# Moving the tiles behind the small triangle by 64 bytes in an attention and feed-forward kernel

## The chip, the cores and the metric

The kernel runs on one core of a Trainium2 chip. The metric is the time of one execution on the device in microseconds; the kernel before was run three times, and the median counts.

## What is computed

Windowed attention with sink tokens over 4 batches of 8 heads, 768 positions and 64 channels, followed by a feed-forward layer over the 3072 tokens that result (512 to 2048 to 512 channels):

```python
scores = scale * np.matmul(q, k.transpose(0, 1, 3, 2))
keep = is_sink | in_window                  # 4 sinks, window 128
scores = np.where(keep, scores, -1000000000.0)
a = np.exp(scores - np.max(scores, axis=-1, keepdims=True))
a = a / (np.sum(a, axis=-1, keepdims=True) + 1e-09)
x = np.matmul(a, v)                         # heads put side by side: [3072, 512]
h = x @ w_in
sp = np.maximum(h, 0.0) + np.log1p(np.exp(-np.abs(h)))
out = (h * erf(sp)) @ w_out
```

## The kernel before

**Tiling.** The tokens are worked on in 12 groups of 256. For each group four pairs of heads go through attention (48 steps), and the result, transposed, is the input of the feed-forward layer: a tile of 128 partitions with 4 blocks of 256 tokens. A group's hidden layer is made in 16 blocks of 128 channels, and each block's activation goes at once into the output product of its group. Attention of later groups is interleaved with the feed-forward work of earlier ones. The order is written out by hand: a loop over slots in which every step has a priority, from a table of offsets, and a few order-only dependencies between instructions of one engine.

**Two kinds of feed-forward products.** The first group is computed in plain float32: `xf` times `wf` (L767) and `gf` times `wf` (L813). From the second group on every operand is split into a high and a low part of a float32 format that TensorE takes in one pass (`F32R`), and three of the four part-products are summed. In the hidden product (L771, 2112 matmuls) the weights `wt` are loaded as the stationary operand, 128 columns of 512 bytes per partition, and 256 columns of `xh` or `xl` stream past them. In the output product (L816, L817, L818, 336 matmuls each) 128 columns of the activation `g` are the stationary operand, and 512 columns of `wt` stream past. A load of the next stationary operand runs beside the matmul before it. Stationary slices begin at multiples of 512 bytes from the start of their tile, and so do the streamed ones.

**Where tiles stand.** A tile pool takes its space at the end of what was opened before, each tile behind the one before it. The weights' pool comes first: 33 buffers of 4096 bytes per partition. Directly behind it stands `pers`, whose first tile is `tri` (the small triangle, a mask of 64 bytes in a tile of 192), then `kq` (11520 bytes), `vz` (8192) and `pst` (4608). Then come the raw inputs (2048, and three of 1536), then the pool `work`: four buffers `u` of 2048, two of `pa` with 2560, two of `pz` with 2048, two of `xh` (and `xf`) with 4096, `r` with 2048, two of `g` (and `gf`) with 4096 and two of `xl` with 4096; at the end the small pool of sums. All pieces from `kq` to `xl` are multiples of 64 bytes.

**Around the change.** `tri` is written once by two compares on VectorE at the start and read by `copy_predicated` in every step's scores. From step 15 on the probabilities go through memory for their transposition: `turn` (in the weights' pool) to `pd` to `pa` (L498), four transfers a step in pieces of 32 elements, issued by SyncE; GpSimd then prepares `pa` and `pz` (L509, L513, L522), and TensorE multiplies them with the values (L563).

Of the kernel before, what the change touches and what calls it, by code (L numbers as in the profile page):

```python
# [19 lines left out]
P = 128  # L20
# [42 lines left out]
def kernel(  # L63
# [74 lines left out]
    def fast_path():  # L138
        with ExitStack() as st:
            pers = st.enter_context(tc.tile_pool(name="pers", bufs=1))  # L140
# [40 lines left out]
            set_mask(mask0)  # L181
            set_mask(mask1)

            tri = pers.tile([P, 192], mybir.dt.int8, name="tri")[:, :64]
            nc.vector.tensor_scalar(tri[:64], rf[:64, :64], float(P), None, op0=ALU.is_ge)
            nc.vector.tensor_scalar(tri[64:], rf[64:, 64:128], float(P), None, op0=ALU.is_lt)

# [637 lines left out]
    def general_path():  # L825

        NT_S = S // P
        with ExitStack() as st:
# [71 lines left out]
            with tc.tile_pool(name="g_one1", bufs=1) as one, tc.tile_pool(name="g_work1", bufs=2) as work:  # L900
# [3 lines left out]
                with tc.For_i(0, B, 1) as b:  # L904
                    for gb in range(GPB):
# [25 lines left out]
                        for i in range(2):  # L931
# [3 lines left out]
                            )  # L935

    fast_path()
    ok = nc.values_load(flagi[0:1, 0:1], min_val=0, max_val=1)
    with tc.If(ok == 0):
# [31 lines left out]
```

## Time and profile before

| | us |
|---|---|
| median of three runs | 712.26 (711.40 to 714.54) |
| the profiled execution | 710.78 |
| its span, first to last instruction | 708.8 |
| TensorE busy | 681.0 (96%) |
| TensorE weight loads busy | 564.1 (80%) |
| VectorE busy | 550.0 (78%) |
| ScalarE busy | 494.0 (70%) |
| GpSimd busy | 297.8 (42%) |
| mean granted clock of TensorE | 0.992 |

A share of busy time is a mean over the span. The stage up to 100 us loads the inputs and works on the first group in plain float32; from there to about 640 us attention and feed-forward work are mixed, and the rest is feed-forward work alone. Weight loads overlap matmuls, and a matmul's length runs from its start to the modelled end of its pipeline; so matmuls overlap as well, and the distance between two starts is shorter than a matmul's length.

### The profile page before, as it was taken

What the parts mean: (1) busy time and instruction counts of PE and PEld (TensorE: products, weight loads), DVE (VectorE), ACT (ScalarE), POOL (GpSimd) and SP (SyncE); (2) the same over time, 40 slices, a digit from 0 to 9 for tenths busy, and PEclk for the clock granted to TensorE, in tenths of its full rate; (3) what the DMA queues carried; (4) which work ended last, traced back from release to release, by engine and by line L of the source; (5) the groups of instructions that cost most, each with busy time, mean ns of one, the idle gap of its engine ahead of it and who ended that gap; (6) DMA issues with size and microseconds to landing.
All of it is one profiled execution on the core that took longest, in us unless ns stands there. A gap on an engine that the chain in (4) does not pass through costs nothing. (4 is left out here: it accounts for less than half of the span.)

```text
span 708.8 us, 16156 instructions
## 1 busy us (share of the span) xinstructions
PE 681.0 (96%) x5515; PEld 564.1 (80%) x5515; DVE 550.0 (78%) x1473; ACT 494.0 (70%) x1157; POOL 297.8 (42%) x501
## 2 busy tenths in 40 slices
PE   6789999999999999899999999999999999999997
PEld 3566566687888888788788888888888888889895
DVE  6979998787889889788898588788798687754352
ACT  4777777986984867476677586686578567586572
POOL 3512410234445545554555455455464337342221
PEclk9989999999999999999999999999999999999999
DMA  7999410202216454653564354453553543220001
GB/s 174 296 325 318 177 31 17 63 16 50 63 35 121 108 113 94 139 102 73 123 119 83 71 122 82 99 120 75 119 103 78 101 95 71 44 68 1 30 1 35
DMA packets 246858, 70.10 MB, mean 99 GB/s; under 512 B 214704, under 2 KB 238896, under 8 KB 246768
## 3 DMA queue, kind: packets, MB, share of 16 engines
q1 hardware_dynamic: 246208, 68.92, 41.8%
q8 instruction: 46, 0.75, 0.4%
q14 instruction: 44, 0.36, 0.2%
q10 hardware_dynamic: 560, 0.07, 0.1%
HBM read 50.27 MB, written 18.42 MB: 97 GB/s over the span
## 5 line engine op out<-in xcount | busy, mean ns | idle before, releaser
L771 PE MATMUL h<-xh,wt 128*128 128x256 f32 x1408 | 271.2, 283 | 1.2 <-DVE u L793 1.2
L771 PEld LDWEIGHTS h<-xh,wt 128*128 128x128 f32 x1408 | 223.4, 188 | 15.6 <-issue 7.8
L771 PE MATMUL h<-xl,wt 128*128 128x256 f32 x704 | 197.0, 280 | 0.3 <-DVE xl L583 0.3
L801 POOL TENSOR_TENSOR g<-u,g 128x512 fp32r<-128x512 f32 x84 | 113.6, 1353 | 176.4 <-DVE g L800 161.5
L789 ACT ACTIVATE u<-r 128x512 f32<-128x512 f32 x288 | 163.3, 623 | 20.4 <-DMA out_dram<-ot 5.5
L793 DVE SCALAR_TENSOR_TENSOR u<-u,u 128x512 f32<-128x512 f32 x168 | 136.2, 811 | 14.5 <-ACT u L789 1.4
L771 PEld LDWEIGHTS h<-xl,wt 128*128 128x128 f32 x704 | 132.4, 188 | 7.0 <-issue 2.8
L816 PE MATMUL o<-wt,g 128*128 128x512 f32 x336 | 133.2, 396 | 0.7 <-DVE g L800 0.6
L817 PE MATMUL o<-wt,g 128*128 128x512 f32 x336 | 132.2, 393 | 0.0
L818 PE MATMUL o<-wt,g 128*128 128x512 f32 x336 | 129.4, 396 | 1.7 <-POOL g L801 1.5
L426 ACT ACTIVATE pst<-pst,neg 128x144 f32<-128x144 f32 x192 | 77.4, 405 | 65.3 <-DVE neg L422 65.2
L793 DVE SCALAR_TENSOR_TENSOR u<-u,h 128x512 f32<-128x512 f32 x84 | 56.7, 675 | 50.6 <-ACT u L789 46.3
L784 ACT ACTIVATE r<-h 128x512 f32<-128x512 f32 x96 | 56.9, 593 | 45.3 <-PE h L771 34.4
L522 POOL TENSOR_SCALAR_AFFINE_SELECT pz<-pa 64x256 f32<-64x256 f32 (+1 forms) x96 | 47.5, 495 | 67.3 <-ACT pa L484 66.0
L816 PEld LDWEIGHTS o<-wt,g 128*128 128x128 f32 x336 | 63.1, 188 | 14.5 <-ACT u L789 1.3
L818 PEld LDWEIGHTS o<-wt,g 128*128 128x128 f32 x336 | 61.8, 188 | 15.9 <-POOL g L801 3.0
L817 PEld LDWEIGHTS o<-wt,g 128*128 128x128 f32 x336 | 63.1, 188 | 10.3 <-issue 0.3
L786 ACT ACTIVATE r<-r 128x512 f32<-128x512 f32 x96 | 60.6, 631 | 2.7
L785 ACT ACTIVATE r<-r 128x512 f32<-128x512 f32 x96 | 60.6, 632 | 2.5
L800 DVE CAST g<-u 128x512 fp32r<-128x512 f32 x84 | 37.5, 447 | 25.0 <-PE o L818 21.5
L513 POOL COPY pz<-pa 64x256 f32<-64x256 f32 x66 | 31.9, 484 | 56.3 <-DMA pa<-pd 55.5
L522 POOL TENSOR_SCALAR_AFFINE_SELECT pa<-pa 64x256 f32<-64x256 f32 (+1 forms) x96 | 47.7, 497 | 4.9
(99 smaller groups left out, 915.1 us busy)
## 6 DMA issues: line engine op xcount, KB each, us to landing
pd<-turn SPq DMA_DIRECT2D x33, 320.0 KB, 2.6
pa<-pd SPq DMA_DIRECT2D x132, 80.0 KB, 2.6
ws<-in_moe_w_in_dram SPq DMA_DIRECT2D x16, 512.0 KB, 6.0
ws<-in_moe_w_out_dram SPq DMA_DIRECT2D x16, 512.0 KB, 8.6
out_dram<-ot SPq DMA_DIRECT2D x24, 256.0 KB, 2.4
v<-in_v_dram SPq DMA_DIRECT2D x56, 96.0 KB, 2.5
kq<-in_k_dram SPq DMA_DIRECT2D x144, 32.0 KB, 2.0
kq<-in_q_dram SPq DMA_DIRECT2D x144, 32.0 KB, 2.2
```

What stands on the lines that cost most here:

```text
L426: mark["e", s] = nc.scalar.activation(y, y, AF.Exp, bias=d["neg"][:, i, h : h + 1], scale=-1.0, accum_out=d["sum"][:, i, h : h + 1])
L522: nc.gpsimd.affine_select(out=out, in_=x, pattern=[[0, 2], [0, 2 - i0], [-sg, HP]], compare_op=op, fill=0.0, base=0, channel_multiplier=sg,)
L771: last = nc.tensor.matmul(o, wt[NC * j + c][:, p, fs], xt[e][:, c, :], start=(m == 0), stop=(m == len(ops) - 1))
L784: nc.scalar.activation(r, h, AF.Tanh, bias=b_t, scale=0.5)
L785: nc.scalar.activation(r, r, AF.Square, bias=b_v, scale=-0.5)
L786: nc.scalar.activation(r, r, AF.Square, bias=b_r)
L789: sq = nc.scalar.activation(u, r, AF.Square, bias=b_a[i], scale=CS)
L793: pr = nc.vector.scalar_tensor_tensor(out=acc, in0=u, scalar=CC[i] * CS**2, in1=x, op0=ALU.add, op1=ALU.mult)
L801: nc.gpsimd.tensor_tensor(gl, acc, gh.bitcast(F32), op=ALU.subtract)
L816: behind(nc.tensor.matmul(o, gh[:, ws], wt[16 + f][:, 0, :], start=(f == 0), stop=False))
L817: nc.tensor.matmul(o, gh[:, ws], wt[16 + f][:, 1, :], start=False, stop=False)
L818: nc.tensor.matmul(o, gl[:, ws], wt[16 + f][:, 0, :], start=False, stop=(f == NF - 1))
```

## The change

The tile that holds the small triangle takes 256 bytes per partition in place of 192. The slice that is used of it stays the first 64 bytes. All tiles behind it stand 64 bytes further on; the weights' buffers, which lie ahead of it, stay.

```diff
-            tri = pers.tile([P, 192], mybir.dt.int8, name="tri")[:, :64]
+            tri = pers.tile([P, 256], mybir.dt.int8, name="tri")[:, :64]
```

## Rows read from the trace of the kernel before

**Rows 1.** The page's busy time: engine, us, share of span, instructions.
```profile
PE 681.0 (96%) x5515; PEld 564.1 (80%) x5515; DVE 550.0 (78%) x1473; ACT 494.0 (70%) x1157; POOL 297.8 (42%) x501
```

**Rows 2.** Busy time by stage, with granted clock, DMA share and GB/s behind.
```profile
100.00:200.00 100.00, 97.16 (x728) 75.04 (x727) 81.05 (x216) 83.20 (x195) 29.62 (x52) 1.00 0.17 40
...
400.00:500.00 100.00, 100.00 (x881) 87.25 (x878) 81.39 (x229) 72.17 (x169) 50.45 (x87) 1.00 0.46 96
...
600.00:700.00 100.00, 100.00 (x734) 88.52 (x733) 52.92 (x111) 63.97 (x121) 29.02 (x31) 1.00 0.11 27
```

**Rows 3.** TensorE's waits, longest first: us in total, times, longest us.
```profile
PE av L563 <- POOL pa L522: 5.2, 6, 1.9
PE tqk L351 <- DMA k_early<-in_k_dram: 4.4, 2, 3.8
```

**Rows 4.** Instructions of L767 and L813: shortest, median, longest ns, first and last start.
```profile
L767 PE MATMUL h<-xf,wf x128: 379/379/796, 25.8 to 93.6; 128*128 128x256 f32 x128
...
L813 PE MATMUL o<-wf,gf x96: 590/592/697, 53.9 to 147.4; 128*128 128x512 f32 x96
```

**Rows 5.** TensorE in order of time near 70 us: start us, us together, instruction.
```profile
69.83 1.67 PE L767 MATMUL h<-xf,wf 128*128 128x256 f32 x7
```

**Rows 6.** Instructions of L771, as in rows 4.
```profile
L771 PEld LDWEIGHTS h<-xh,wt x1408: 186/188/192, 102.8 to 694.2; 128*128 128x128 f32 x176
L771 PE MATMUL h<-xh,wt x1408: 276/278/683, 102.8 to 694.4; 128*128 128x256 f32 x176
...
L771 PE MATMUL h<-xl,wt x704: 276/278/388, 103.3 to 694.2; 128*128 128x256 f32 x176
```

**Rows 7.** TensorE in order of time, a hidden product at 383 us.
```profile
382.71 0.39 PE L771 MATMUL h<-xh,wt 128*128 128x256 f32 x2
...
383.73 0.28 PE L771 MATMUL h<-xh,wt 128*128 128x256 f32 x1
```

**Rows 8.** TensorE in order of time, a hidden product at 652 us.
```profile
651.69 0.40 PE L771 MATMUL h<-xh,wt 128*128 128x256 f32 x2
...
652.75 0.28 PE L771 MATMUL h<-xh,wt 128*128 128x256 f32 x1
```

**Rows 9.** Groups by line, 651.46 to 652.5 us: busy us, mean ns, idle before.
```profile
L771 PE MATMUL h<-xh,wt 128*128 128x256 f32 x6 | 1.2, 281 | 0.0
...
L771 PEld LDWEIGHTS h<-xh,wt 128*128 128x128 f32 x6 | 0.9, 190 | 0.0
```

**Rows 10.** Instructions of L816, L817 and L818, as in rows 4.
```profile
L816 PEld LDWEIGHTS o<-wt,g x336: 186/188/192, 156.1 to 702.7; 128*128 128x128 f32 x168
L816 PE MATMUL o<-wt,g x336: 388/390/505, 156.2 to 703.0; 128*128 128x512 f32 x168
...
L817 PEld LDWEIGHTS o<-wt,g x336: 186/188/193, 156.2 to 703.0; 128*128 128x128 f32 x168
L817 PE MATMUL o<-wt,g x336: 388/392/505, 156.4 to 703.2; 128*128 128x512 f32 x168
...
L818 PE MATMUL o<-wt,g x336: 388/394/503, 156.6 to 703.4; 128*128 128x512 f32 x168
```

**Rows 11.** TensorE in order of time, an output product at 308 us.
```profile
306.64 0.39 PE L816 MATMUL o<-wt,g 128*128 128x512 f32 x1
...
309.39 0.28 PE L771 MATMUL h<-xh,wt 128*128 128x256 f32 x1
```

**Rows 12.** TensorE in order of time, an output product at 162 us.
```profile
161.05 0.40 PE L816 MATMUL o<-wt,g 128*128 128x512 f32 x1
...
163.15 0.39 PE L817 MATMUL o<-wt,g 128*128 128x512 f32 x1
```

**Rows 13.** Two last matmuls of a sequence by line, and the loads behind them.
```profile
L818 PE MATMUL o<-wt,g 128*128 128x512 f32 x1 | 0.4, 388 | 0.0
301.95 0.53 PEld L563 LDWEIGHTS av<-pa,v 128*64 128x64 f32 x12 [2.38 <-POOL pa L522]
...
L818 PE MATMUL o<-wt,g 128*128 128x512 f32 x1 | 0.4, 397 | 0.0
330.84 0.42 PEld L563 LDWEIGHTS av<-pa,v 128*64 128x64 f32 x8 [0.36 <-issue]
```

**Rows 14.** The page's DMA issues: KB each, median us to landing.
```profile
pa<-pd SPq DMA_DIRECT2D x132, 80.0 KB, 2.6
```

## The prediction

> **What bounds the kernel now.** I read the share of busy time first, then the table by stage, then TensorE's waits. TensorE is busy for 681.0 of the 708.8 us of the span, the next engine for 550.0 [rows 1]; from 100 us on it is busy for 97 to 100 us of every 100, at the full granted clock of 1.00, which is the 2.4 GHz level [rows 2]. Its longest wait by name adds up to 5.2 us in six pieces [rows 3]. So the time is the number of matmuls times the distance from one start to the next, and what a start-to-start gains or loses is passed on almost whole. The change touches no instruction. It can only act through how long an instruction takes on operands that stand 64 bytes further on.
>
> **Where the operands stand.** The 33 weight buffers have 4096 bytes each, so all start at one place modulo 512, and the small triangle's tile follows directly behind them, at that same place. From there to the feed-forward inputs it is 192 bytes for the triangle, 11520 (kq), 8192 (vz), 4608 (pst), 2048 and 4608 (the raw tiles), 8192 (u), 5120 (pa), 4096 (pz): 48576 = 95 x 512 - 64. The hidden product's moving inputs xh and xl, and the output product's stationary tile g, thus stand 64 bytes short of the weights' place; with 256 in place of 192 they stand on it. What each product reads beside what changes from -64 to 0 (inputs streaming past weights) and from +64 to 0 (weights streaming past g).
>
> **What the two products cost now.** I measure against plain float32 on the same engine: 256 columns take 379 ns and 512 take 592 [rows 4], 213 ns for 256 columns, and seven such matmuls in 1.67 us start (1670 - 379) / 6 = 215 ns apart [rows 5]. The split products pass a column in half that time, so without any stall 512 columns would take 379 ns and start 215 ns apart, 256 would take 379 - 107 = 272.
> The hidden product takes 276 ns at its shortest, 278 in the median [rows 6]. It runs at one of two even paces for many matmuls in a row: nine starts in 383.73 - 382.71 = 1.02 us, 113.3 ns each, and nine in 652.75 - 651.69 = 1.06 us, 117.8 each [rows 7, 8]; in the second the matmul itself lasts 281 and the loads of xh's weights 190 in the mean instead of 188 [rows 9]. The median halfway between 276 and 281 says that each pace has about half of the 2112 matmuls. The faster pace is above what 256 columns need, since a load of 128 columns takes as long as they do and only starts with the matmul before; it is the floor here. The slower pace costs 4.5 ns x 1056 = 4.8 us.
> The output product's three lines take 388 at the shortest and 390, 392 and 394 in the median [rows 10]. Twelve start in 309.39 - 306.64 = 2.75 us, 229.2 ns each; in another stretch nine in 163.15 - 161.05 = 2.10 us, 233.3 each [rows 11, 12]. Over the unstalled 215 that is 14 ns each, 14.1 us for 1008 matmuls. So some 19 us of the span are stalls of reading. Whether those come from the place is the whole question.
>
> **The change, part by part.** Removed and added: no instruction, no wait, no transfer. The triangle's own two writes and the predicated copies read 64 bytes as before: nothing.
>
> Place of an operand taken by itself. The hidden product's stationary operand stands on the weights' place, the output product's 64 bytes short of it, and both load in 188 ns in the median, between 186 and 193 [rows 6, 10]. In plain float32 the moving operand stands 64 bytes short (xf) or on the place (wf), and 592 is 379 + 213 without a remainder [rows 4]. By these rows the place alone costs nothing. For the split products the rows have each moving operand at one place only, and the excess per 256 columns is 4 to 9 ns at either (276 and 281 over 272 there; 388 and 397 over 379 for twice the columns here). I take 0; the ends are in the next step.
>
> Place of two operands to one another, when a load runs beside a matmul. This no row shows at another distance than 64. Two rows bear on it from the side: matmuls that end a sequence, beside which no load runs. One took 388 ns, with no load for 2.38 us; another took 397, with no load for 0.36 us [rows 13]. Matmuls with a load beside them take 388 at the shortest and 390 to 394 in the median [rows 10], so they are no longer. So most of the stall is there without the neighbour that the change would move, and I take 0. Against it speaks the slower pace, where the load is lengthened too, 190 for 188 [rows 9]: the two streams do meet somewhere. So both ends stay open: below, all 19 us gone; above, the slowest paces seen everywhere, 4.5 ns for the other 1056 hidden matmuls (4.8 us) and 233.3 - 229.2 = 4.1 ns for 1008 output matmuls (4.1 us), 8.9 us.
> The Trainium skill, TensorE: Matmul & The Clock Gate, Part 2, says that the streamed operand and the weight load have a read port each and that loading takes nothing from the running matmul. By that rule the relative place is worth 0; the matmuls without a load beside them agree with it (388 and 397), the lengthened load of the slower pace does not.
>
> Tiles that transfers write. The transposed probabilities (pa), the raw inputs and the copies of the values move by 64 bytes as well, and SyncE's queue issues the same transfers in the same order. A pa transfer lands in 2.6 us in the median [rows 14], behind it GpSimd prepares the tile, and TensorE waits for that for 5.2 us in all [rows 3]. If landing gets shorter, at most those 5.2 us are to be had; the same 5.2 us taken again is my bound for a loss. I take 0, because six waits in 33 steps mean that the transfer is nearly always early.
> [...]
>
> Vector, scalar and GpSimd work keeps its shapes; its tiles move together, and only weight splitting and the turn tile meet an operand that stays. TensorE's 97 to 100 of 100 us cover it; if that cover went, DVE's 550.0 us [rows 1] have 131 us of room.
>
> **Sum.** 0 against the profiled execution's 710.78 us, whose span is 708.8 with 2.0 around it. The median of the runs is 712.26, 1.5 above that execution, so the forecast is 712.3.
>
> **The rivals.**
> *Slower: inputs and weights collide.* On one place, the streams of a matmul and of the next load begin together on the same part of each 512 bytes. If that makes the slower paces the rule, the price is the 8.9 us above: 721.2. It decides as soon as a hidden matmul can no longer stay at 113.3 ns. For it: two paces exist, and the slow one lengthens both streams. Against it: the stall without a load.
> *Faster: the collisions are there now and end.* If the distance of 64 bytes is what throws hidden matmuls to 117.8, its end gives back 4.8 us, and the output product at its shortest of 388 instead of about 392 gives 4 ns x 1008 = 4.0 us: 703.5. All stalls gone would be 712.3 - 18.9 = 693.4. For it: the 14 ns that every output matmul pays. Against it: the same lengths without a load, and plain float32 pays nothing at the same distance of 64.
> *Faster through the transfers.* At most 5.2 us: 707.1. For it: every piece starts at another address; against it: the rare waits.
> *The change does not do what it says*: buffers could be laid out with other gaps, or the order of instructions could shift. Nothing in the code rests on the triangle's width, so this comes to the forecast's time.
>
> **How the numbers follow.** No change, with the last case in it: 0.38, 709 to 716. Slower through collisions: 0.32, around 721. Faster through their end: 0.27, 693 to 707; through transfers: 0.03. The range reaches from 700, which leaves out the outer half of the faster case, to 724, some us above the slow case: about 8 in 10. Chances: faster by over 0.5% 0.30, within 0.5% 0.38, slower by over 0.5% 0.32; half a per cent, 3.6 us, is about what a measurement of this kernel can tell from no change.
>
> **What would show it.** Right: 276 and 281 both remain in the hidden product, with a median between them, and 388 to 397 in the output product, loads at 188. Collisions: a hidden median of 281 or more, loads above 190, output medians above 394. Collisions ended: a hidden median of 276, output matmuls near 379. Transfers: TensorE's wait for pa falls from 5.2 us. The forecast is wrong if start-to-start paces of 113.3, 117.8, 229.2 and 233.3 give way to others: then place matters in a way that no row of before shows.

## The result and the profile after

The changed kernel takes 716.33 us in the median of six runs (715.95 to 717.78), the kernel before 711.95 beside it; the ratio is 1.0052, with a 95% interval of 1.0035 to 1.0069. So the change makes the kernel slower by half a per cent, 4.4 us by the medians. The profiled execution of the changed kernel took 717.06 us, its span 715.0, against 708.8 of before. No instruction changed its place in the order on any engine.

The busy time of the page, as in [rows 1]:

```profile
PE 687.7 (96%) x5515; PEld 572.2 (80%) x5515; DVE 552.5 (77%) x1473; ACT 493.5 (69%) x1157; POOL 296.0 (41%) x501
```

TensorE is busy for 6.7 us more and its loads for 8.1 us more, with the same counts; VectorE, ScalarE and GpSimd stay within 3 us. The clock does not differ where the split products run: from 100 to 700 us the granted clock is 1.00 in both traces. Which instructions became longer is seen in the views of one line: shortest, median and longest ns, as in [rows 6, 10].

```profile
L771 PEld LDWEIGHTS h<-xh,wt x1408: 185/192/193, 104.4 to 700.3; 128*128 128x128 f32 x176
L771 PE MATMUL h<-xh,wt x1408: 276/283/682, 104.4 to 700.5; 128*128 128x256 f32 x176
...
L771 PE MATMUL h<-xl,wt x704: 274/283/387, 105.0 to 700.3; 128*128 128x256 f32 x176
...
L816 PE MATMUL o<-wt,g x336: 387/395/505, 158.1 to 709.1; 128*128 128x512 f32 x168
...
L817 PE MATMUL o<-wt,g x336: 387/393/499, 158.4 to 709.3; 128*128 128x512 f32 x168
...
L818 PE MATMUL o<-wt,g x336: 387/389/505, 158.6 to 709.6; 128*128 128x512 f32 x168
```

In the hidden product both went up: the load from 188 to 192 ns in the median, the matmul from 278 to 283. In the output product the three lines changed places (390, 392, 394 became 395, 393, 389), and their sum stayed within 1 ns. How it looks in order of time, where [rows 7, 8] showed two paces:

```profile
654.40 0.40 PE L771 MATMUL h<-xh,wt 128*128 128x256 f32 x2
...
655.48 0.28 PE L771 MATMUL h<-xh,wt 128*128 128x256 f32 x1
```

Nine distances from start to start in 655.48 - 654.40 = 1.08 us are 120.0 ns each, an even pace that the rows of before do not show. In that stretch the loads take 192 ns in the mean, and the matmuls 283:

```profile
L771 PEld LDWEIGHTS h<-xh,wt 128*128 128x128 f32 x7 | 1.1, 192 | 0.0
...
L771 PE MATMUL h<-xh,wt 128*128 128x256 f32 x7 | 1.4, 283 | 0.0
```

I worked out the mean distance between two starts from all hidden matmuls whose successor starts within 130 ns: 115.65 ns over 2039 of them before, 119.42 over 2040 after. That is 3.77 x 2040 = 7.7 us. For the output product (successor within 260 ns) it is 230.09 before and 230.08 after.

From the first start of a hidden matmul to the last it is 694.4 - 102.8 = 591.6 us before [rows 6] and 700.5 - 104.4 = 596.1 after: 4.5 us more, not 7.7. Most of the rest came back from waits. TensorE's waits after the change, over the whole span, as in [rows 3]:

```profile
PE tqk L351 <- DMA k_early<-in_k_dram: 5.0, 2, 3.8
PE h L767 <- DVE gf L793: 4.0, 1, 4.0
PE av L563 <- POOL pa L522: 3.5, 5, 2.1
...
PE o L818 <- POOL g L801: 0.2, 1, 0.2
```

Over the whole span the wait for pa fell from 5.2 to 3.5 us, but 0.9 of this lies ahead of the first split product. Between the first and the last hidden start, TensorE's waits for pa and for the low part of g were these before:

```profile
PE av L563 <- POOL pa L522: 3.4, 4, 1.9
PE o L818 <- POOL g L801: 1.5, 4, 0.6
```

And after:

```profile
PE av L563 <- POOL pa L522: 2.6, 3, 2.1
...
PE o L818 <- POOL g L801: 0.2, 1, 0.2
```

That is 2.1 us less in these two; all waits of TensorE in this stretch add up to 8.6 us before and 5.9 after, 2.7 less. A slower TensorE comes later to what GpSimd makes, which would shorten such waits, but this reason is not shown: the kernel below with all tiles moved, whose TensorE is not slower, waits 2.8 and 0.8 us in the two, and the one with a tile of 320 bytes, whose TensorE is, 2.7 and 1.5. So part of the 2.1 us may be spread between executions.

The remaining 1.6 us of the span's 6.2 lie ahead of the first split product (102.8 against 104.4). In the profiled executions below that start lies between 102.2 and 104.1 us without an order by place, so I count it as spread as well; the medians, 4.4 us apart, agree with the 4.5.

### The profile page after: what moved, and what is told of

The parts are those of the page before. It is cut to its first block, busy times and chain, and to the rows that moved or that the text cites. A ratio compares the mean times of both kernels' runs of the same rounds, so it can differ in the third digit from the quotient of the medians.

```text
span 715.0 us, 16156 instructions
## 1 busy us (share of the span) xinstructions
PE 687.7 (96%) x5515; PEld 572.2 (80%) x5515; DVE 552.5 (77%) x1473; ACT 493.5 (69%) x1157; POOL 296.0 (41%) x501
## 5 line engine op out<-in xcount | busy, mean ns | idle before, releaser
L771 PE MATMUL h<-xh,wt 128*128 128x256 f32 x1408 | 278.9, 287 | 1.0 <-DVE u L793 1.0
L771 PEld LDWEIGHTS h<-xh,wt 128*128 128x128 f32 x1408 | 227.4, 191 | 15.4 <-issue 7.8
L771 PE MATMUL h<-xl,wt 128*128 128x256 f32 x704 | 199.9, 284 | 0.2 <-DVE xl L583 0.2
L771 PEld LDWEIGHTS h<-xl,wt 128*128 128x128 f32 x704 | 134.4, 191 | 6.8 <-issue 2.8
L816 PE MATMUL o<-wt,g 128*128 128x512 f32 x336 | 133.6, 398 | 0.5 <-DVE g L800 0.5
L817 PE MATMUL o<-wt,g 128*128 128x512 f32 x336 | 132.3, 394 | 0.0
L818 PE MATMUL o<-wt,g 128*128 128x512 f32 x336 | 128.4, 393 | 0.6 <-POOLq L939 0.2
L816 PEld LDWEIGHTS o<-wt,g 128*128 128x128 f32 x336 | 63.5, 189 | 14.4 <-ACT u L789 1.3
L818 PEld LDWEIGHTS o<-wt,g 128*128 128x128 f32 x336 | 62.0, 188 | 14.9 <-POOL g L801 1.6
L817 PEld LDWEIGHTS o<-wt,g 128*128 128x128 f32 x336 | 63.5, 189 | 9.7 <-issue 0.3
L422 DVE CUSTOM_DVE_ANT_0 pst<-ps,mask 128x144 f32<-128x144 f32 x192 | 47.5, 304 | 1.5
```

Source lines behind the costliest of these rows:

```text
L771: last = nc.tensor.matmul(o, wt[NC * j + c][:, p, fs], xt[e][:, c, :], start=(m == 0), stop=(m == len(ops) - 1))
L816: behind(nc.tensor.matmul(o, gh[:, ws], wt[16 + f][:, 0, :], start=(f == 0), stop=False))
L817: nc.tensor.matmul(o, gh[:, ws], wt[16 + f][:, 1, :], start=False, stop=False)
L818: nc.tensor.matmul(o, gl[:, ws], wt[16 + f][:, 0, :], start=False, stop=(f == NF - 1))
```

## The experiments

The kernel before ran again beside each group of runs: 711.23 us in the median of 24 beside the kernels up to `g` alone, 711.42 in the median of 17 beside the others. The ratios are against these.

**TensorE alone, at every distance.** A kernel that does nothing of the computation: 40 matmuls in a row of the hidden product's shape with the inputs at 0 to 512 bytes past the weights' place, then the same for the output product's shape.

```python
for d in range(0, 513, 16):                     # then downwards
    for m in range(40):
        matmul(o[:, :256], wt[:, m % 8 * 128 : m % 8 * 128 + 128], xs[:, d // 4 : d // 4 + 256])
for d in range(0, 513, 32):
    for m in range(40):
        matmul(o, xs[:, m % 2 * 128 + d // 4 : ...], wt[:, m % 2 * 512 : m % 2 * 512 + 512])
```

> TensorE alone, nothing of the kernel's computation is done: 40 matmuls in a row of the hidden product's shape for each distance from the weights' place to the inputs' place, 0 to 512 bytes in steps of 16, upwards and downwards, then the output product's shape in steps of 32. Pair theory (loads and stream of a hidden matmul meet in memory, and how much depends on their distance): 448 (64 short, as before) shows a start-to-start of 113 to 118 ns, 0 shows 119 to 120 with loads of 192 ns, 512 is like 0; the output shape shows 229 to 234 at both places. Rival (the change acts elsewhere, through transfers or other engines' operands): all distances show one pace, within 1 ns, as nothing else runs here.

TensorE in order of time: start, us of all 40 together, and the distance spelled in digits in the tile's name (hid: inputs past weights; out: g past weights):

```profile
20.22 4.96 PE L67 MATMUL hidzerozerozero<-xs,wt 128*128 128x256 f32 x40
...
39.17 4.87 PE L67 MATMUL hidzerosixfour<-xs,wt 128*128 128x256 f32 x40
43.88 4.95 PE L67 MATMUL hidzeroeightzero<-xs,wt 128*128 128x256 f32 x40
...
53.46 4.72 PE L67 MATMUL hidoneonetwo<-xs,wt 128*128 128x256 f32 x40
58.02 4.90 PE L67 MATMUL hidonetwoeight<-xs,wt 128*128 128x256 f32 x40
...
76.96 4.72 PE L67 MATMUL hidoneninetwo<-xs,wt 128*128 128x256 f32 x40
...
95.72 4.95 PE L67 MATMUL hidtwofivesix<-xs,wt 128*128 128x256 f32 x40
...
114.65 4.87 PE L67 MATMUL hidthreetwozero<-xs,wt 128*128 128x256 f32 x40
...
152.45 4.72 PE L67 MATMUL hidfourfoureight<-xs,wt 128*128 128x256 f32 x40
...
331.86 9.26 PE L79 MATMUL outzerozerozero<-wt,xs 128*128 128x512 f32 x40
...
350.28 9.50 PE L79 MATMUL outzerosixfour<-wt,xs 128*128 128x512 f32 x40
...
387.60 9.33 PE L79 MATMUL outoneninetwo<-wt,xs 128*128 128x512 f32 x40
...
461.81 9.33 PE L79 MATMUL outfourfoureight<-wt,xs 128*128 128x512 f32 x40
```

The length of 40 goes with the distance although no other engine works, and it repeats after 256 bytes: 0 and 256, 64 and 320, 192 and 448 agree to a hundredth of a microsecond. At the place of before (448, which is 192) the hidden shape takes the least, together with 112; the place after the change (0) is among the longest, with 80 and 96 beside it. The granted clock is 1.00 in all these stretches. The last 20 starts of each stretch are 113.3 ns apart at 192 and 448, 117.8 at 64 and 320, 120.0 at 0, 256 and 512; among the 16-byte steps only 112 and 192 (and 256 more) reach 113.3, the others lie between 116.5 and 120.2. Some of these differ between the way up and the way down (128: 118.6 and 120.0), 0, 64, 112 and 192 do not. For the output shape it is the other way round at 0: 226.7 ns there, 229.1 at 192, 232 to 234 elsewhere, where I had put 229 to 234 at both places. The loads at 0, 80 and 448 (shortest, median, longest):

```profile
L67 PEld LDWEIGHTS hidzerozerozero<-xs,wt x40: 188/192/192, 20.0 to 24.8; 128*128 128x128 f32 x40
...
L67 PEld LDWEIGHTS hidzeroeightzero<-xs,wt x40: 187/188/192, 43.8 to 48.4; 128*128 128x128 f32 x40
...
L67 PEld LDWEIGHTS hidfourfoureight<-xs,wt x40: 187/188/192, 152.3 to 156.8; 128*128 128x128 f32 x40
```

So the pace of 120 ns with its loads of 192 arises in TensorE alone, with no other engine at work. The load's length is not what makes every slow pace: at 80 bytes the 40 matmuls take 4.95 us with loads of 188.

**All tiles moved, the weights too.** Is it the inputs' place or their distance from the weights?

```diff
-    tiny = cpool.tile([P, 16], F32, name="tiny")
+    tiny = cpool.tile([P, 32], F32, name="tiny")
```

> The weights' buffers move by 64 bytes too (a constant ahead of them is 64 bytes larger), so the inputs stand where the change puts them, and still 64 bytes short of the weights. Pair theory: the time of before, 712 us, hidden matmuls at 278 ns in the median and loads at 188. Rival (the inputs' own place modulo 512 counts): the time after, 716 us, hidden median 283, loads 192. Rival (the moved tiles of transfers and other engines): 716 as well, with the hidden rows of before.

710.41 us in the median, ratio 0.9979 (0.9961 to 0.9997): not slower. The hidden product is in its old paces:

```profile
L771 PEld LDWEIGHTS h<-xh,wt x1408: 186/188/330, 102.2 to 693.9; 128*128 128x128 f32 x176
L771 PE MATMUL h<-xh,wt x1408: 276/280/683, 102.2 to 694.0; 128*128 128x256 f32 x176
```

The mean from start to start is 115.77 ns (before 115.65). Every tile behind the triangle stood where the change puts it, and the time of before stayed, so the inputs' place by itself, the transfers into moved tiles and the place of the other engines' operands by itself are out.

**The hidden product's inputs, without g.** `r` and `g` are allotted first and keep their place modulo 512 bytes; a tile of 64 bytes behind them moves xh, xl and the other work tiles.

```diff
+            work.tile([P, 512], F32, tag="r", bufs=1, name="r_first")
+            work.tile([P, 2, 512], F32, tag="g", bufs=2, name="g_first")
+            work.tile([P, 16], F32, tag="pad", bufs=1, name="pad")
             ri = work.tile([P, 512], I32, tag="u", bufs=UB, name="ri")
```

> Only the activation g and its scratch r stay at their old place; xh, xl and all other work tiles move by 64 bytes onto the weights' place. Pair theory in the hidden product: 716 us, hidden median 283 ns, loads 192, output rows as before (390, 392, 394). Rival (the output product pays): 712 us.

716.24 us, ratio 1.0071 (1.0046 to 1.0096): the whole loss of the change. The tiles `u`, `pa` and `pz` moved too, but the loss stands in the hidden rows. The hidden line, three lines further down in this kernel:

```profile
L774 PE MATMUL h<-xh,wt x1408: 274/283/682, 103.7 to 700.1; 128*128 128x256 f32 x176
```

Its mean from start to start is 119.64 ns, with loads of 189 in the median (not the 192 expected: the pace of 120 is reached by two thirds of the matmuls, and 124 or 117 by the rest).

**The output product's g alone.** xh and xl are allotted first, and `r`, which stands ahead of `g`, gets 64 bytes more.

```diff
+            for t in "hl":
+                work.tile([P, NC, GT], F32R, tag="x" + t, name=f"x{t}_first")
...
-            r = work.tile([P, 512], F32, tag="r", bufs=1, name=f"r_{m}")
+            r = work.tile([P, 528], F32, tag="r", bufs=1, name=f"r_{m}")[:, :512]
```

> Only g moves by 64 bytes onto the weights' place; xh, xl and all else stay. Pair theory in the hidden product: 711 to 712 us, hidden median 278 ns, loads 188; output rows like those after the change (395, 393, 389), worth 0 in sum. Rival (the output product pays): 716 us.

711.9 us, ratio 1.0003 (0.9982 to 1.0024): no loss, as the pair theory had it. But the rows within are not those that I expected:

```profile
L773 PE MATMUL h<-xh,wt x1408: 276/281/684, 103.7 to 697.3; 128*128 128x256 f32 x176
...
L818 PE MATMUL o<-wt,g x336: 387/389/504, 157.0 to 705.9; 128*128 128x512 f32 x168
```

The output product became faster (389 ns in all three lines' medians; from start to start 227.95 instead of 230.09, 2.2 us for 1008), and the hidden product, whose operands did not move, became slower (115.65 to 116.48 from start to start, 1.8 us for 2112): the part of its matmuls in the pace of 113 fell from 0.52 to 0.31. My reading is that the output product hands TensorE over to the next hidden matmuls at another moment, and that they then stay in the pace of 117.8 more often; the last experiment bears on it.

**Other distances in the kernel: 192 bytes short, 64 past, 128 short.** Three kernels differ from before in the triangle's tile alone.

```diff
-            tri = pers.tile([P, 192], mybir.dt.int8, name="tri")[:, :64]
+            tri = pers.tile([P, 64], mybir.dt.int8, name="tri")[:, :64]     # 320 and 128 in the others
```

> The triangle's tile takes 64 bytes: all inputs stand 192 bytes short of the weights. By the pace table (distance 320 and 64 alike: hidden 117.8 ns, output 233.4) the hidden product costs (117.8 - 115.65) x 2112 = 4.5 us more than before and the output product (233.4 - 230.1) x 1008 = 3.3 us: about 719 us. If the period is 256 bytes, it equals the tile of 320 bytes within 1 us; if it is 512, the two differ. Rival (any place but the old one collides as the change does): 716 with loads of 192 ns; here loads stay at 188.

> The triangle's tile takes 320 bytes: all inputs stand 64 bytes past the weights, 256 bytes from the place of the tile of 64 bytes. Period 256: the same time and paces as there, about 719 us, hidden pace 117.8 ns, loads 188. Period 512 or a rule by closeness: nearer to 716, loads lengthened.

> The triangle's tile takes 128 bytes: all inputs stand 128 bytes short. By the pace table (hidden 118.7 to 119.9 ns, output 232.4) the hidden product costs 6.4 to 9 us more than before and the output product 2.3: 719 to 722 us. If only standing on one place (modulo 256) costs, it is the time of before, 711 to 712.

With 64 bytes 715.37 us, ratio 1.0060 (1.0036 to 1.0084); with 320 bytes 716.35, 1.0067 (1.0047 to 1.0086); with 128 bytes 716.78, 1.0077 (1.0054 to 1.0100). The hidden loads of the kernel with 64, then the hidden line and the first output line of the kernels with 64 and with 320, in this order:

```profile
L771 PEld LDWEIGHTS h<-xh,wt x1408: 186/188/193, 104.1 to 700.3; 128*128 128x128 f32 x176
L771 PE MATMUL h<-xh,wt x1408: 276/279/687, 104.1 to 700.4; 128*128 128x256 f32 x176
...
L816 PE MATMUL o<-wt,g x336: 390/394/505, 157.6 to 709.0; 128*128 128x512 f32 x168
```

```profile
L771 PE MATMUL h<-xh,wt x1408: 276/279/687, 103.5 to 700.4; 128*128 128x256 f32 x176
...
L816 PE MATMUL o<-wt,g x336: 390/394/505, 157.0 to 709.0; 128*128 128x512 f32 x168
```

The two agree in these rows, and in their means from start to start (117.65 and 117.70 for the hidden product, 233.37 and 233.38 for the output product): the period of 256 bytes holds in the kernel. The hidden line with 128:

```profile
L771 PE MATMUL h<-xh,wt x1408: 274/282/684, 102.3 to 699.5; 128*128 128x256 f32 x176
```

Its means are 119.08 and 232.12 ns. The paces are those of the table (at 128 bytes 118.6 to 120.0 and 232.0), but the times are less than I expected, 715 to 717 instead of 719 to 722. By their times alone the kernels with 64 and with 320 bytes came out where the rivals had put them, at 716; what speaks against those rivals is that the loads stay at 188 and that the two kernels have one set of paces. That only standing on one place costs is refuted by the kernel with 128 bytes, which would have kept the time of before. The stalls add up to 2.0 x 2112 + 3.3 x 1008 = 7.6 us in the first two, while from the first hidden start to the last it is 596.3 and 596.9 us, 4.7 and 5.3 more than before: again only a part of the stalls reaches the time, as in the changed kernel.

**Both products in turn, TensorE alone.** Nothing of the computation is done; 24 hidden matmuls in the kernel's order and 12 of the output product, four such rounds for each of 48 pairs of places.

```python
for x0 in (0, 112, 192):
    for g0 in range(0, 256, 16):
        for r in range(4):
            hidden(x0, 0); hidden(x0, 1); output(g0, 0); output(g0, 1)
```

> TensorE alone, nothing of the kernel's computation is done: the real order of both products (24 hidden matmuls with xh, xl, xh, then 12 of the output product), for inputs 0, 112 and 192 bytes past the weights' place and g at every 16 bytes of 256. Pair theory: the round of 36 takes least with inputs at 192 and longest at 0, by some (119.6 - 115.7) x 24 = 94 ns; with inputs at 192, g at 0 gains the output product 12 x 2 ns but hands the hidden product over in its slower pace, so that the sum is within 10 ns of g at 192. If the hand-over plays no part, g at 0 wins by 24 ns a round, and inputs at 112 equal those at 192.

The first matmul of three of the pairs, and of the pair behind each: inputs and g at 0 (the change), inputs at 192 and g at 0 (g moved alone), both at 192 (before). The long names lose their first letters:

```profile
20.20 0.28 PE L74 MATMUL erozerozerogzerozerozero<-xh,wt 128*128 128x256 f32 x1
...
42.69 0.28 PE L74 MATMUL xzerozerozerogzeroonesix<-xh,wt 128*128 128x256 f32 x1
...
737.30 0.28 PE L74 MATMUL xoneninetwogzerozerozero<-xh,wt 128*128 128x256 f32 x1
...
759.42 0.28 PE L74 MATMUL hxoneninetwogzeroonesix<-xh,wt 128*128 128x256 f32 x1
...
1004.10 0.28 PE L74 MATMUL hxoneninetwogoneninetwo<-xh,wt 128*128 128x256 f32 x1
...
1026.06 0.28 PE L74 MATMUL xoneninetwogtwozeroeight<-xh,wt 128*128 128x256 f32 x1
```

A quarter of each difference is one round: 5.62 us at the places of the change, 5.53 with g alone moved, 5.49 at those of before. In the round of before a hidden matmul starts 114.3 ns after the other and an output matmul 229.0; with g at 0 it is 116.9 and 227.0, so what the output product gains, (229.0 - 227.0) x 12 = 24 ns, the hidden product loses twice over, (116.9 - 114.3) x 24 = 62. I had put the sum within 10 ns; it is 39 worse. Over the 16 places of g a round takes 5.65 us in the mean with inputs at 0 and 5.56 with inputs at 112 or 192, about the 94 ns that I had put. The places of before are the best of the 48, with inputs at 112 and g at 16 next (5.50 us).

That the pace also depends on what ran before shows within one pair, inputs at 192 and g at 176. Its four rounds are the same instructions on the same operands and with the same output buffers; each starts here:

```profile
981.90 0.28 PE L74 MATMUL hxoneninetwogonesevensix<-xh,wt 128*128 128x256 f32 x1
...
987.40 0.28 PE L74 MATMUL hxoneninetwogonesevensix<-xh,wt 128*128 128x256 f32 x1
...
993.00 0.28 PE L74 MATMUL hxoneninetwogonesevensix<-xh,wt 128*128 128x256 f32 x1
...
998.50 0.28 PE L74 MATMUL hxoneninetwogonesevensix<-xh,wt 128*128 128x256 f32 x1
```

The next pair starts at 1004.10, so the rounds take 5.50, 5.60, 5.50 and 5.60 us in turn.

No version came out of this that would beat the kernel before, and none was run.

## Why the prediction was right and wrong

**The forecast's time and its range.** The forecast was no change, 712.3 us, with 700 to 724 around it. The measured 716.33 lies in the range, 0.3 us past the 709 to 716 that I had given to no change. It is in the range because the range reached up for the slower rival; the mechanism that I stated for the forecast did not hold.

**The step that failed: "Place of two operands to one another ... I take 0."** The runs put it at 7.7 us of hidden start-to-start, of which 4.4 reached the time. I took the matmuls without a load beside them, 388 and 397 ns [rows 13], as evidence that the stall does not come from the neighbour. Those are two output matmuls, and they say little about the hidden product. For the output product they misled as well: its starts gave back 2.2 us with g alone moved, and cost 3.3 us more with all inputs 192 bytes short. That they came to 0.0 under this change is luck. TensorE alone shows the two parts of it: with g at 0 output matmuls start 227.0 ns apart when the inputs stand at 192, and 229.0, as at the places of before, when they stand at 0. [rows 9] had the sign of the hidden loss, loads of 190 in place of 188 in the slow pace; I named that row and gave it too little weight. The Trainium skill, SBUF — State Buffer, SBUF: two separate sides, says that TensorE never waits on anyone. If this is meant of its own two streams too, the runs disagree: with no other engine at work a load takes 192 ns against 188 by the distance alone.

**"The place alone costs nothing."** Right: with all tiles and the weights moved together the time of before stayed (0.9979). One of the reasons that I gave for it was empty, though: 213 ns is 592 - 379, so that 592 is 379 + 213 tests nothing; only the 215 ns from start to start is a second measurement.

**The rival "Slower: inputs and weights collide".** Its direction and its marks are what the runs show: a hidden median above 281 (283) and loads above 190 (192). Its reason is not. It had the streams meet on one place of each 512 bytes, but 192 and 128 bytes short and 64 past cost as much (715.4 to 716.8 us), and the period is 256 bytes. Of its price of 8.9 us both terms were mis-sized. The hidden term was 4.8 us, with the slowest pace of before as its end; the new pace of 120.0 lies beyond it, and the term came to 7.7. The output term was 4.1 and came to 0.0: medians above 394 came in one line of three. And of the 7.7 us only 4.4 reached the time.

**"What a start-to-start gains or loses is passed on almost whole."** Too simple: 57% was passed on (4.4 of 7.7). TensorE's waits between the first and the last hidden start fell by 2.7 us, most of it in pa and g. [rows 3] showed the wait for pa, and I did not set it against the slow case. How much of the fall a slower TensorE causes is open, as said above.

**The rivals "Faster".** The 64 bytes were not what throws hidden matmuls to 117.8; they are one of two distances in a period at which they can run at 113.3 at all. About half of the hidden matmuls of before are at 117.8 all the same, and what ran before them has a part in it: with g alone moved the share at 113 fell from 0.52 to 0.31. Transfers of pa land in 2.6 us as before, and with all tiles moved together the time changed by 0.4% at most, so the place of what the transfers write is worth next to nothing.

What remains open: why some distances cost and others do not, and whether the load or the stream is what waits. The runs show the period of 256 bytes and the paces at each 16 bytes, no rule behind them. Matmuls without any load beside them at other places were not measured.

## What to carry to other kernels

In a product like this hidden one, 256 streamed columns with a load of 128 beside them, the distance between streamed operand and stationary operand modulo 256 bytes belongs to the design: write down both, and measure a table of 40 matmuls in a row at every 16 bytes before a tile ahead of them is resized. Where two products take turns, measure them in turn as well, since the pace of one depends on the other. A change to any tile in the same pool can move that distance, here by 64 bytes of padding for half a per cent. Do not carry a row of one product over to another, and set a loss on the busiest engine against its own waits before passing it on.

## What was not expected of the hardware

Matmuls of the split format (`F32R`) settle into even paces: 113.3, 117.8 and 120.0 ns for 256 columns at the distances 192, 64 and 0, with the load of the next stationary operand at 188, 188 and 192. Which pace a sequence takes depends on the distance of the operands modulo 256 bytes, and, at a distance with more than one, on what ran before it: the same round of both products takes 5.50 and 5.60 us in turn. Plain float32 matmuls keep 379 ns in the median at the place after the change too, and their loads 190:

```profile
L767 PEld LDWEIGHTS h<-xf,wf x128: 186/190/338, 26.3 to 95.0; 128*128 128x128 f32 x128
L767 PE MATMUL h<-xf,wf x128: 378/379/797, 26.3 to 95.2; 128*128 128x256 f32 x128
```
